# The fourth GEMM's operands as float16 pairs from the second token group on

## The chip, the core and the metric

The kernel runs on one NeuronCore of a Trainium2 chip. TensorE multiplies, VectorE, ScalarE and GpSimd (POOL) do the elementwise work, and SyncE's queue (SP) issues every DMA. The metric is the device time of one execution in microseconds: before the change 741.53 us, the median of three runs (739.75 to 742.87).

## The reference

The computation is one attention block and two feed-forward blocks behind it, on 2304 tokens:

```python
out = attention(q_l, k_l, v_l, q_g, k_g, v_g)        # 4 batches, 8 heads of 64: 512 local tokens with a window of 32, 32 global ones
x   = out as (2304, 512)
h   = x @ w_in                                        # GEMM 1, (512, 1024)
s   = h * softmax(h);  ln = (s - mean) / sqrt(var + 1e-6) * g_ln
x   = ln @ w_out                                      # GEMM 2, (1024, 512)
h   = x @ w2_in                                       # GEMM 3, (512, 2048)
g   = h * clip(h + 3, 0, 6) / 6
out = g @ w2_out                                      # GEMM 4, (2048, 512)
```

All inputs are float32, and the weight matrices come as 64-bit words of which the kernel takes out the float32 values on chip ("decoding").

## The kernel before

**Numbers as pairs.** GEMMs 1 to 3 are done in float16 with each operand as a pair: a high half (the value, scaled by a power of two and rounded) and a low half (the rest). A product takes three passes: high by high, high by low, low by high. GEMM 4 works in the same three passes with pairs of float32r, which need no scale: the pair of `w2_out` (tile w2o, made in `prep_w2` by L887 and L354) and the pair of g (tile gr, made by L914 and L916).

**Tiling.** The tokens are 17 tiles of 128. The last two GEMMs (`second`) run over five groups of 4, 4, 3, 3 and 3 tiles, and in each group over 16 blocks f of 128 of the 2048 hidden columns. For a block, GEMM 3 puts 12 matmuls (3 passes by 4 parts of the depth, L906, 512 or 384 moving columns) into one of two PSUM banks S. From there ScalarE makes the clipped factor (L910), VectorE the product g (L912), ScalarE the high half (L914), VectorE the low half (L916). GEMM 4 (L925) then takes 3 passes by 4 or 3 token tiles, each a matmul with 512 moving columns, into four banks (V_71, V_72, Y_74, Y_75) that collect over all 16 blocks. At the end of a group the banks are scaled by 1/6 (L939 on VectorE, L941 on ScalarE) and written out.

**Weights.** `prep_w2` decodes a block's part of `w2_in` and of `w2_out`. A block of words lands in one of three buffers raw, is taken apart by ScalarE (L404) and VectorE or GpSimd (L410 to L422) into one of five buffers wd (for four early blocks into the memory zone), and is split. The scale of `w2_in` comes from a sum of squares on ScalarE (L428, `norm`, which writes its squares into a tile junk) and a matmul of one column with a matrix of ones (L372, into bank H, `power_scale`), behind which VectorE cuts out the exponent (L368 to L370) and makes the block's factor (L879, tile inv). A block's words come in behind one another through raw, so the decoding of 16 blocks runs beside the end of GEMMs 1 and 2 and beside group 0.

**Order.** A planner (`Plan.schedule`) fixes the order of all instructions on all engines. It takes each operation's cost from formulas such as `dve` and `act`, starts what can start earliest and, among what starts within 0.05 us, the operation of lowest rank. Decoding has ranks up to 56, group 0 from 100 to 118, group 1 from 120 on. A region (the memory of a stage) may be used once the operations of the regions named by `closes` are done. Each engine then runs its list in order: a waiting instruction holds up all that stand behind it on its engine.

## Time and profile before

| | us |
|---|---|
| median of three runs | 741.53 |
| the profiled execution | 739.12 |
| its span, first to last instruction | 737.3 |
| TensorE busy | 681.0 (92%) |
| VectorE busy | 435.4 (59%) |
| ScalarE busy | 391.2 (53%) |
| GpSimd busy | 161.9 (22%) |

Busy times are from the profile's page. Matmuls are pipelined, so their listed durations overlap, and a busy TensorE says only that something was in flight. How fast it goes is read from starts: from the start of one matmul, or of one run of them, to that of the next. The attention and GEMM 1 take the first half; from about 374 us to the end TensorE works on GEMMs 3 and 4, group 0 to about 455 us.

### The profile page before, as it was taken

To read this page: it belongs to the slowest core of one execution; us is meant where nothing else is said; L and a number is where in the kernel's file an instruction comes from. 1 tells how busy PE (TensorE), PEld (TensorE's weight loads), DVE (VectorE), ACT (ScalarE), POOL (GpSimd) and SP (SyncE) were. 2 spreads that over 40 slices of the span, in tenths; PEclk is the share of its full clock that TensorE was granted. 3 is DMA by queue.
4 is the path that set the end of the run, shared out by engine and by line. 5 is a ranking of instruction groups with operands and counts; after the bars stand their busy time and mean duration, and the time that the engine had idled before them with its cause. 6 is when DMAs were issued, how large, how long until landed. Compare 5 with 4: busy or idle time off the path is not lost.

```text
span 737.3 us, 11841 instructions
## 1 busy us (share of the span) xinstructions
PE 681.0 (92%) x4484; PEld 466.2 (63%) x4484; DVE 435.4 (59%) x1052; ACT 391.2 (53%) x736; POOL 161.9 (22%) x192
## 2 busy tenths in 40 slices
PE   3667599999989999898999999999999999999997
...
DVE  4898977877757988868789962231232232223222
...
PEclk9977759999999999999999999999999999999999
...
GB/s 319 243 252 169 217 152 184 156 214 186 224 218 166 183 227 161 146 141 138 177 65 154 125 29 57 1 1 0 1 58 1 0 44 1 0 1 44 1 0 44
DMA packets 155657, 82.93 MB, mean 112 GB/s; under 512 B 132944, under 2 KB 141136, under 8 KB 155600
## 3 DMA queue, kind: packets, MB, share of 16 engines
...
## 4 chain that ended last, share of the span: by engine, by line
PE 70%; DMA 12%; DVE 10%; issue 2%; ACT 2%; SPq 2%; POOL 1%; ACTq 0%; DVEq 0%
PE S L906 20%; PE V L925 14%; PE Y L925 9%; PE Y L852 8%; PE H L792 7%; DMA PT<-zone 7%; PE S L601 5%; PE S L636 2%; DMA lT<-l 2%; PE V L728 2%; DMA vs<-v 2%; DVE wd L417 1%; DMA zone<-in_ki_dram 1%; DVE wd L410 1%; PE V L678 1%
## 5 line engine op out<-in xcount | busy, mean ns | idle before, releaser
L925 PE MATMUL V<-w2o,gr 128*128 128x512 f32 x480 | 155.5, 408 | 0.2 <-ACT gr L914 0.2
L912 DVE SCALAR_TENSOR_TENSOR g<-g,S 128x384 f32<-128x384 f32 (+1 forms) x80 | 48.3, 606 | 158.7 <-ACT g L910 156.5
L906 PE MATMUL S<-ybig,w2i 128*128 128x384 f16 (+1 forms) x720 | 139.7, 348 | 0.5 <-DVE g L912 0.5
L910 ACT ACTIVATE g<-S,three,inv 128x384 f32<-128x384 f32 (+1 forms) x80 | 57.0, 712 | 156.0 <-PE S L906 153.6
L925 PE MATMUL Y<-w2o,gr 128*128 128x512 f32 x336 | 116.0, 397 | 0.0
L906 PEld LDWEIGHTS <-w2i 128*128 128x128 f16 x720 | 67.6, 98 | 65.0 <-issue 10.4
L925 PEld LDWEIGHTS V<-w2o,gr 128*128 128x128 f32 x480 | 88.4, 188 | 23.7 <-ACT gr L914 3.5
L852 PE MATMUL Y<-lT,wout 128*128 128x256 f16 (+1 forms) x864 | 96.6, 269 | 4.5 <-DMA lT<-l 3.2
L792 PE MATMUL H<-win,xT 128*128 128x512 f16 x384 | 91.9, 387 | 0.2 <-DVE tm L805 0.2
L852 PEld LDWEIGHTS <-wout 128*128 128x128 f16 x864 | 79.9, 99 | 18.2 <-DMA lT<-l 4.0
L916 DVE SCALAR_TENSOR_TENSOR gr<-g,inv,gr 128x384 fp32r<-128x384 f32 (+1 forms) x80 | 53.7, 671 | 47.6 <-ACT gr L914 33.2
L914 ACT ACTIVATE gr<-g,inv 128x384 fp32r<-128x384 f32 (+1 forms) x80 | 52.4, 657 | 44.2 <-DVE g L912 44.0
L925 PEld LDWEIGHTS Y<-w2o,gr 128*128 128x128 f32 x336 | 63.2, 188 | 15.5 <-DVE gr L916 0.2
L792 PEld LDWEIGHTS <-xT 128*128 128x128 f16 x384 | 36.6, 100 | 42.5 <-issue 6.6
L601 PE MATMUL S<-zone 64*128 64x224 f32 x256 | 57.4, 454 | 4.9 <-ACT sg L642 4.3
L611 ACT ACTIVATE e<-e,sa 128x224 f32<-128x224 f32 x128 | 52.7, 471 | 9.3 <-DVE sa L606 9.2
L601 PEld LDWEIGHTS S<-zone 64*128 64x128 f32 x256 | 38.8, 230 | 16.2 <-ACT sg L642 6.0
L606 DVE CUSTOM_DVE_ANT_0 e<-msk,S 128x224 f32<-128x224 f32 x128 | 43.1, 382 | 8.6 <-PE S L601 8.3
L906 PE MATMUL S<-ybig,zone 128*128 128x384 f16 (+1 forms) x240 | 47.1, 348 | 0.0
L678 PE MATMUL V<-v,PT 128*128 128x65 f16 x128 | 25.8, 205 | 18.9 <-DMA PT<-zone 18.8
L636 PE MATMUL S<-zone 128*128 128x128 f32 (+1 forms) x128 | 28.0, 352 | 11.6 <-DVE sa L606 11.6
L626 DVE SCALAR_TENSOR_TENSOR zone<-e,zone 128x896 f16<-128x896 f32 x32 | 34.6, 1084 | 3.1 <-ACT zone L624 2.8
(181 smaller groups left out, 1032.2 us busy)
## 6 DMA issues: line engine op xcount, KB each, us to landing
...
```

The source lines that it names most:

```text
L601: T.matmul(out=S()[:, j], lhsT=p.tile(qk)[d, 2 * hf + j], rhs=p.tile(kk)[d, 2 * hf + j], start=True, stop=True)
L606: V.tensor_tensor_reduce(out=p.tile(ek)[:, KC * (2 * j + jj):KC * (2 * j + jj) + KC], in0=msk[:, mtyp], in1=S()[:, j], scale=-0.125, scala ...
L611: A.activation(out=p.tile(ek)[:, c:c + KC], in_=p.tile(ek)[:, c:c + KC], func=AF.Exp, bias=p.tile(sa)[:, h:h + 1], scale=-1.0)
L636: T.matmul(out=p.tile(gk)[:, 0:n], lhsT=p.tile(gq)[:, 2 * hf + j], rhs=p.tile(kk)[:, 2 * hf + j, 0:n], start=(j == 0), stop=(j == 1))
L792: T.matmul(out=p.tile(hk)[:, 512 * n:512 * n + 512], lhsT=(p.tile(xk) if xb else xgT)[:, 4 * a + k], rhs=win16[:, w, k, 512 * n:512 * n + ...
L852: T.matmul(out=Y()[:, m2], lhsT=wout16[:, w, k, 128 * m:128 * m + 128], rhs=p.tile(lk)[:, 8 * a + k, 0:n], start=(z == 0 and k == 0), stop ...
L906: T.matmul(out=p.tile(hk)[:, 0:n], lhsT=p.tile(wk)[:, w, k], rhs=y16[:, a, k, c0:c0 + n], start=(z == 0 and k == 0), stop=(z == 2 and k == 3))
L910: aop(act(n, 2), lambda hk=hk, gk=gk, iv=iv: A.activation(out=p.tile(gk)[:, 0:n], in_=p.tile(hk)[:, 0:n], func=AF.Relu, bias=three, scale= ...
L912: vop(dve(n), lambda hk=hk, gk=gk: V.scalar_tensor_tensor(out=p.tile(gk)[:, 0:n], in0=p.tile(gk)[:, 0:n], scalar=6.0, in1=p.tile(hk)[:, 0: ...
L914: aop(act(n, 1, sbuf=True), lambda rk=rk, gk=gk, iv=iv: A.activation(out=p.tile(rk)[:, 0, 0:n], in_=p.tile(gk)[:, 0:n], func=AF.Copy, scal ...
L916: vop(dve(n, 1), lambda rk=rk, gk=gk, iv=iv: V.scalar_tensor_tensor(out=p.tile(rk)[:, 1, 0:n], in0=p.tile(gk)[:, 0:n], scalar=iv[:, 0:1], ...
L925: T.matmul(out=p.tile(accs[t]), lhsT=p.tile(rk)[:, a, 128 * t:128 * t + 128], rhs=p.tile(ok)[:, w], start=(f == 0 and z == 0), stop=(f == ...
```

## The change

Group 0 stays as it is. From group 1 on GEMM 4 works in float16 pairs: the weights from new tiles wh, and g from a new tile gh, whose two halves are made by the same two instructions as before.

For that, `prep_w2` takes one more sum of squares on ScalarE for each block of `w2_out`. `token_scale` makes one scale for g out of two columns that GEMM 1's normalisation now keeps (lsq, lfac). `convert_scale` adds the 16 sums, sends them through one more matmul with ones and makes 16 factors. `convert` turns each block's float32r pair into a float16 pair: the high half on ScalarE, the rest in two steps on VectorE, of which the first writes over the high float32r half and so stands behind group 0's use of it. The pairs go into the memory of the decoding (raw, wd, four parts of the zone, junk), which is free when the last block is decoded. Outputs of groups 1 to 4 are scaled by a column (inv6) instead of a constant, and there is one output buffer less.

```diff
-    tags(const, "raw", SLOTS["raw"], [128, 1024], F32)
-    tags(const, "wd", SLOTS["wd"], [128, 512], F32)
+    tags(const, "raw", SLOTS["raw"], [128, 1024], F32, "r")
+    tags(const, "wd", SLOTS["wd"], [128, 512], F32, "r")
...
-        carve(f"wz{f}", 1, [128, DM], F32, "z")
+        carve(f"wz{f}", 1, [128, DM], F32, "zr")
...
+    halves = [t[:, z:z + DM] for t in p.slots["raw"]["tiles"] for z in (0, 512)] + [t[:, 0:DM] for t in p.slots["wd"]["tiles"]]
+    halves += [t for f in range(SLOTS["EARLY"], SLOTS["EARLY"] + SLOTS["ZONE"]) for t in p.slots[f"wz{f}"]["tiles"]]
+    halves = [t.bitcast(F16) for t in halves] + [junk.bitcast(F16)]
+    for f in range(NF):
+        p.tag(f"wh{f}", [halves[f].rearrange("p (a n) -> p a n", a=2)], "c")
...
         aop(act(512, sbuf=True), lambda: A.activation(out=p.tile(o2)[:, 0], in_=p.tile(d2), func=AF.Copy), r=[d2], w=[("w2oh", f)], b=[d2, o2], rank=rank + 0.05)
+        norm(lambda: p.tile(d2), am_w2o[:, f:f + 1], [d2, ("inv3", f)], "amw2o", rank + 0.06, [d2], scale=ivk[:, 0:1])
...
+    def token_scale(rank):
+        t = const.tile([128, NU + 1], F32, name="tsc")
+        si = g_scale.bitcast(I32)
+        pk = p.buf("tsc", "H")
+        x = t[:, 0:NU]
+        steps = [
+            lambda: V.scalar_tensor_tensor(out=x, in0=lfac, scalar=2.0 ** -30, in1=lfac, op0=ALU.mult, op1=ALU.mult),
+            lambda: V.tensor_tensor(out=x, in0=x, in1=lsq, op=ALU.mult),
+            lambda: V.tensor_tensor(out=x, in0=x, in1=x, op=ALU.mult),
+            lambda: V.tensor_tensor(out=x, in0=x, in1=x, op=ALU.mult),
+            lambda: V.tensor_reduce(out=t[:, NU:NU + 1], in_=x, axis=AX.X, op=ALU.add),
+        ]
...
+        pe(0.12, lambda: T.matmul(out=p.tile(pk)[:, 0:1], lhsT=ones, rhs=t[:, NU:NU + 1], start=True, stop=True), r=prev, w=["tsc5"], b=[pk], rank=rank)
...
+    def convert_scale(rank):
+        vop(dve(NF), lambda: V.tensor_reduce(out=am_w2o[:, NF:NF + 1], in_=am_w2o[:, 0:NF], axis=AX.X, op=ALU.add), r=["amw2o"], w=["amw2o1"], rank=rank)
+        s = power_scale(lambda: am_w2o[:, NF:NF + 1], ["amw2o1"], "s_w2o", rank, "H")
+        vop(0.07, lambda: V.tensor_scalar(out=inv6, in0=s[:, 1:2], scalar1=g_scale[:, 1:2], scalar2=1.0 / 6.0, op0=ALU.mult, op1=ALU.mult), r=["s_w2o", "g_scale"], w=["inv6"], rank=rank)
+        for f in range(NF):
+            vop(0.13, lambda f=f: V.tensor_scalar(out=inv3[f][:, 1:2], in0=inv3[f][:, 0:1], scalar1=s[:, 0:1], scalar2=None, op0=ALU.mult), r=["s_w2o", ("inv3", f)], w=[("wt", f)], rank=rank + 0.1 * f)
+
+    def convert(f, rank):
+        ok = ("w2o", f)
+        hk = p.buf(("wh", f), f"wh{f}")
+        iv = inv3[f]
+        done = [("o", 0, f, 2)] if f < NF - 1 else [("oo", 0, t) for t in range(GROUPS[0][1])]
+        aop(act(512, 1, sbuf=True), lambda: A.activation(out=p.tile(hk)[:, 0], in_=p.tile(ok)[:, 0].bitcast(F32), func=AF.Copy, scale=iv[:, 1:2]),
+            r=[ok, ("wt", f)], w=[("whh", f)], b=[ok, hk], rank=rank)
+        vop(dve(512, 1), lambda: V.scalar_tensor_tensor(out=p.tile(ok)[:, 0], in0=p.tile(ok)[:, 0].bitcast(F32), scalar=iv[:, 1:2], in1=p.tile(hk)[:, 0], op0=ALU.mult, op1=ALU.subtract),
+            r=[("whh", f)] + done, w=[("wht", f)], b=[ok, hk], rank=rank)
+        vop(dve(512, 1), lambda: V.scalar_tensor_tensor(out=p.tile(hk)[:, 1], in0=p.tile(ok)[:, 1].bitcast(F32), scalar=iv[:, 1:2], in1=p.tile(ok)[:, 0].bitcast(F32), op0=ALU.mult, op1=ALU.add),
+            r=[("wht", f)], w=[hk], b=[ok, hk], rank=rank)
...
-            rk = p.buf(("gr", gi, f), "gr")
-            wk, ok = ("w2i", f), ("w2o", f)
+            rk = p.buf(("gr", gi, f), "gh" if gi else "gr")
+            wk, ok = ("w2i", f), ("wh" if gi else "w2o", f)
...
+            gs, own = (g_scale[:, 0:1], ["g_scale"]) if gi else (iv[:, 0:1], [])
...
+            sc, ptr, need = (inv6, 1, ["inv6"]) if gi else (1.0 / 6.0, 0, [])
...
     for gi in range(len(GROUPS)):
         second(gi)
+        if gi == 0:
+            token_scale(100.0)
+            convert_scale(115.9)
+            for f in range(NF):
+                convert(f, 118.0 + f)
...
-    p.schedule({"g": ["a"], "h": ["m"], "z": ["s"]})
+    p.schedule({"g": ["a"], "h": ["m"], "z": ["s"], "zr": ["s"], "c": ["r", "zr"]})
...
-            shapes = {"g": ([128, 512], F32), "gr": ([128, 2, 512], F32R), "o": ([128, DM], F32)}
+            shapes = {"g": ([128, 512], F32), "gr": ([128, 2, 512], F32R), "gh": ([128, 2, 512], F16), "o": ([128, DM], F32)}
```

The planner makes a new order for all engines. Up to about 320 us TensorE's and VectorE's lists are as before. On ScalarE, in the decoding of the last blocks, stood before, between the sums of squares for the `w2_in` scales of blocks 14 and 15 (inv_14, inv_15; w2o_4214 is block 14's pair, g and gr are the steps of blocks 11 and 12):

```order
L428 ACTIVATE junk,inv_14_202<-wd_90 128x512
L887 ACTIVATE w2o_4214<-wd_86 128x512
L910 ACTIVATE g_3517<-S_69,three,inv_12_198 128x512
L441 ACTIVATE wd_90<-wd_90,psc_203 128x512
L404 ACTIVATE wd_88<-raw_85 128x512
L447 ACTIVATE w2i_3537<-wd_90 128x512
L914 ACTIVATE gr_3521<-g_3519,inv_11_196 128x512
L428 ACTIVATE junk,inv_15_204<-wd_87 128x512
```

and now:

```order
L436 ACTIVATE junk,inv_14_207<-wd_90 128x512
L901 ACTIVATE w2o_4235<-wd_86 128x512
L449 ACTIVATE wd_90<-wd_90,psc_208 128x512
L455 ACTIVATE w2i_3546<-wd_90 128x512
L436 ACTIVATE junk,am_w2o<-wd_86,inv_14_207 128x512
L436 ACTIVATE junk,inv_15_209<-wd_87 128x512
```

The steps of blocks 11 and 12 have moved behind; the new sum of squares of block 14 (into am_w2o) stands in front of block 15's.

On TensorE, around the one-column matmul for block 15's scale (H_73 from inv_15), GEMM 4 of blocks 10 (w2o_4210) and 11 (w2o_4211) stood before:

```order
L925 MATMUL Y_74<-w2o_4210,gr_3520 128x512
L925 MATMUL Y_75<-w2o_4210,gr_3520 128x512
L372 MATMUL H_73<-inv_15_204,ones 128x1
L925 MATMUL V_71<-w2o_4211,gr_3521 128x512
L925 MATMUL V_72<-w2o_4211,gr_3521 128x512
```

and now GEMM 3 of block 13 (w2i_3545) in front of it and GEMM 4 of block 9 (w2o_4230) behind it, with the token scale's matmul:

```order
L968 LDWEIGHTS w2i_3545
L968 MATMUL S_70<-ybig,w2i_3545 128x512
L372 MATMUL H_73<-inv_15_209,ones 128x1
L988 MATMUL V_71<-w2o_4230,gr_3529 128x512
L988 MATMUL V_72<-w2o_4230,gr_3529 128x512
L988 MATMUL Y_74<-w2o_4230,gr_3529 128x512
L988 MATMUL Y_75<-w2o_4230,gr_3529 128x512
L926 MATMUL H_73<-tsc,ones 128x1
```

Twenty matmuls more of GEMM 4 now stand behind that matmul.

On VectorE, at the end of group 0, the steps of blocks 12 to 15 stood before without anything between them (inv_12 to inv_15 name the blocks):

```order
L916 SCALAR_TENSOR_TENSOR gr_3520<-g_3517,inv_12_198,gr_3520 128x512
L912 SCALAR_TENSOR_TENSOR g_3518<-g_3518,S_70 128x512
L916 SCALAR_TENSOR_TENSOR gr_3521<-g_3518,inv_13_200,gr_3521 128x512
L912 SCALAR_TENSOR_TENSOR g_3519<-g_3519,S_69 128x512
L916 SCALAR_TENSOR_TENSOR gr_3520<-g_3519,inv_14_202,gr_3520 128x512
L912 SCALAR_TENSOR_TENSOR g_3517<-g_3517,S_70 128x512
L916 SCALAR_TENSOR_TENSOR gr_3521<-g_3517,inv_15_204,gr_3521 128x512
L912 SCALAR_TENSOR_TENSOR g_3518<-g_3518,S_69 128x512
```

and now, behind the matmul for the common scale, the first conversion (w2o_92 with raw_83 is block 0) and the steps of blocks 14 and 15, with the last two of the 16 factors ahead:

```order
L937 TENSOR_SCALAR inv_14_207<-inv_14_207,psc_212 128x1
L937 TENSOR_SCALAR inv_15_209<-inv_15_209,psc_212 128x1
L946 SCALAR_TENSOR_TENSOR w2o_92<-w2o_92,inv_0_179,raw_83 128x512
L979 SCALAR_TENSOR_TENSOR gr_3528<-g_3527,inv_14_207,gr_3528 128x512
L948 SCALAR_TENSOR_TENSOR raw_83<-w2o_92,inv_0_179 128x512
L974 SCALAR_TENSOR_TENSOR g_3525<-g_3525,S_70 128x512
L946 SCALAR_TENSOR_TENSOR w2o_3548<-w2o_3548,inv_1_181,raw_83 128x512
L946 SCALAR_TENSOR_TENSOR w2o_4223<-w2o_4223,inv_2_183,raw_84 128x512
L979 SCALAR_TENSOR_TENSOR gr_3529<-g_3525,inv_15_209,gr_3529 128x512
L948 SCALAR_TENSOR_TENSOR raw_83<-w2o_3548,inv_1_181 128x512
```

Conversions and the steps of g take turns on VectorE from here to block 4 of group 1.

## Rows read from the trace of the kernel before

**Rows 1.** The page, 40 slices, tenths: TensorE busy, VectorE busy, granted clock.

```profile
PE   3667599999989999898999999999999999999997
...
DVE  4898977877757988868789962231232232223222
...
PEclk9977759999999999999999999999999999999999
```

**Rows 2.** The page, the chain that ended last, by engine.

```profile
PE 70%; DMA 12%; DVE 10%; issue 2%; ACT 2%; SPq 2%; POOL 1%; ACTq 0%; DVEq 0%
```

**Rows 3.** Windows: length, busy us (count) of PE, PEld, DVE, ACT, POOL; clock, DMA, GB/s.

```profile
340.00:350.00 10.00, 7.81 (x43) 4.21 (x41) 9.33 (x21) 6.01 (x10) 3.27 (x4) 0.95 1.07 225
350.00:360.00 10.00, 10.00 (x84) 8.54 (x83) 7.71 (x15) 4.40 (x8) 0.00 (x0) 0.88 0.45 142
...
420.00:430.00 10.00, 10.00 (x46) 6.40 (x46) 9.82 (x19) 7.46 (x14) 3.51 (x3) 1.00 0.19 60
430.00:440.00 10.00, 10.00 (x47) 6.46 (x46) 4.66 (x12) 2.80 (x5) 1.71 (x1) 1.00 0.01 2
```

**Rows 4.** The chain in order of time: start us, us, what.

```profile
360.16 6.11 DMA lT<-l
...
467.86 5.19 PE S L906 x24
478.69 5.20 PE S L906 x24
...
563.19 3.92 PE S L906 x24
571.32 3.92 PE S L906 x24
```

**Rows 5.** Lines by form from 455 us on: busy us, mean ns, idle before.

```profile
L925 PE MATMUL V<-w2o,gr 128*128 128x512 f32 x385 | 124.0, 406 | 0.0
L925 PE MATMUL Y<-w2o,gr 128*128 128x512 f32 x240 | 86.0, 397 | 0.0
...
L925 PEld LDWEIGHTS V<-w2o,gr 128*128 128x128 f32 x384 | 71.0, 188 | 18.3 <-ACT gr L914 2.2 <-ACT o L941 0.3
L906 PEld LDWEIGHTS <-w2i 128*128 128x128 f16 x564 | 53.2, 98 | 46.6 <-issue 6.8
...
L914 ACT ACTIVATE gr<-g,inv 128x512 fp32r<-128x512 f32 x15 | 10.8, 723 | 11.3 <-DVE g L912 11.3
```

**Rows 6.** Timeline, end of group 0: start us, us, engine, line, what.

```profile
453.52 1.57 PE L925 MATMUL V<-w2o,gr 128*128 128x512 f32 x6
```

**Rows 7.** Timeline, TensorE and ScalarE in the decoding.

```profile
423.25 0.63 ACT L428 ACTIVATE junk<-wd 128x512 bf16<-128x512 f32 x1 [0.43 <-DVE wd L419]
...
423.88 0.61 ACT L887 ACTIVATE w2o<-wd 128x512 fp32r<-128x512 f32 x1
...
430.23 0.28 PE L372 MATMUL H<-inv,ones 128*128 128x1 f32 x2
...
430.92 0.63 PE L925 MATMUL Y<-w2o,gr 128*128 128x512 f32 x2
```

**Rows 8.** Waits of TensorE from 320 to 455 us: total, times, longest.

```profile
PE H L372 <- ACT junk L428: 1.8, 2, 1.6
...
PE Y L852 <- DMA lT<-l: 1.3, 2, 0.7
PE S L906 <- DVE g L912: 0.5, 1, 0.5
```

**Rows 9.** Timeline, VectorE at the end of the decoding.

```profile
431.84 0.20 DVE L879 TENSOR_SCALAR inv<-psc,psc 128x1 f32<-128x1 f32 x1
...
431.97 0.68 DVE L419 SCALAR_TENSOR_TENSOR wd<-raw,wd 128x512 int32<-128x512 int32 x1
...
432.57 0.74 DVE L437 SCALAR_TENSOR_TENSOR w2i<-wd,psc,w2i 128x512 f16<-128x512 f32 x1
...
433.23 0.74 DVE L916 SCALAR_TENSOR_TENSOR gr<-g,inv,gr 128x512 fp32r<-128x512 f32 x1
```

More of the change, by code (lines that the diff above doesn't have):

```diff
@@ L774, in passes @@
         return [[(k, a, w) for k in range(n)] for a, w in ((0, 0), (0, 1), (1, 0))]
+    lsq = const.tile([128, NU], F32, name="lsq")
+    lfac = const.tile([128, NU], F32, name="lfac")
     def gemm1(u):
@@ L806, in gemm1 @@
             port=False, r=[("me", u)], w=[("mu", u)], b=[hk, uk, tk], rank=rank)
-        aop(act(1024, 1, 1, True), lambda: A.activation(out=junk, in_=p.tile(uk), func=AF.Square, bias=c(3), scale=-float(DFF), accum_out=c(5)),
+        aop(act(1024, 1, 1, True), lambda: A.activation(out=junk, in_=p.tile(uk), func=AF.Square, bias=c(3), scale=-float(DFF), accum_out=lsq[:, u:u + 1]),
             r=[("mu", u)], w=[("sq", u)], b=[uk, tk], rank=rank)
@@ L814, in gemm1 @@
         tiny(lambda: G.tensor_scalar(out=c(7), in0=c(6), scalar1=c(6), scalar2=1e-6 * DFF * 2.0 ** -10, op0=ALU.mult, op1=ALU.mult), ["c6"], "c7")
-        tiny(lambda: G.tensor_scalar(out=c(8), in0=c(5), scalar1=2.0 ** -30, scalar2=c(7), op0=ALU.mult, op1=ALU.add), ["sq", "c7"], "c8")
-        tiny(lambda: G.tensor_tensor(out=c(9), in0=c(8), in1=mhalf, op=ALU.pow), ["c8"], "y3", 0.5)
+        tiny(lambda: G.tensor_scalar(out=c(8), in0=lsq[:, u:u + 1], scalar1=2.0 ** -30, scalar2=c(7), op0=ALU.mult, op1=ALU.add), ["sq", "c7"], "c8")
+        tiny(lambda: G.tensor_tensor(out=lfac[:, u:u + 1], in0=c(8), in1=mhalf, op=ALU.pow), ["c8"], "y3", 0.5)
         mode = MODE["l"][u]
@@ L824, in gemm1 @@
                r=[("sq", u)], w=[("mc", u)], b=[uk, tk], rank=rank)
-        aop(act(1024, 1, 0, True), lambda: A.activation(out=p.tile(lk)[:, 0], in_=p.tile(uk), func=AF.Copy, scale=c(9)),
+        aop(act(1024, 1, 0, True), lambda: A.activation(out=p.tile(lk)[:, 0], in_=p.tile(uk), func=AF.Copy, scale=lfac[:, u:u + 1]),
             r=[("mc", u), ("y3", u)], w=[("lh", u)], b=[uk, lk, tk], rank=rank)
-        vop(dve(1024, 1), lambda: V.scalar_tensor_tensor(out=p.tile(lk)[:, 1], in0=p.tile(uk), scalar=c(9), in1=p.tile(lk)[:, 0], op0=ALU.mult, op1=ALU.subtract),
+        vop(dve(1024, 1), lambda: V.scalar_tensor_tensor(out=p.tile(lk)[:, 1], in0=p.tile(uk), scalar=lfac[:, u:u + 1], in1=p.tile(lk)[:, 0], op0=ALU.mult, op1=ALU.subtract),
             r=[("lh", u)], w=[lk], b=[uk, lk, tk], rank=rank)
@@ L864, in attention_solu_swish_kernel @@
     w2i, w2o, inv3 = {}, {}, {}
+    am_w2o = const.tile([128, NF + 1], F32, name="am_w2o")
+    inv6 = const.tile([128, 1], F32, name="inv6")
     three = const.tile([128, 1], F32, name="three")
@@ new lines, in token_scale @@
+    def token_scale(rank):
[10 more added lines that the diff above has]
+        ]
+        prev = [("y3", u) for u in range(NU)]
+        for z, fn in enumerate(steps):
+            vop(dve(NU), fn, r=prev, w=[("tsc", z)], rank=rank)
+            prev = [("tsc", z)]
+        pe(0.12, lambda: T.matmul(out=p.tile(pk)[:, 0:1], lhsT=ones, rhs=t[:, NU:NU + 1], start=True, stop=True), r=prev, w=["tsc5"], b=[pk], rank=rank)
+        vop(0.13, lambda: V.tensor_scalar(out=si[:, 2:3], in0=p.tile(pk).bitcast(I32)[:, 0:1], scalar1=26, scalar2=23, op0=ALU.logical_shift_right, op1=ALU.logical_shift_left), port=False, r=["tsc5"], w=["tsc6"], b=[pk], rank=rank)
+        vop(0.07, lambda: V.tensor_scalar(out=si[:, 0:1], in0=si[:, 2:3], scalar1=-1.0, scalar2=float(128 << 23), op0=ALU.mult, op1=ALU.add), r=["tsc6"], w=["g_scale"], rank=rank)
+        vop(0.07, lambda: V.tensor_scalar(out=si[:, 1:2], in0=si[:, 2:3], scalar1=1.0, scalar2=float(126 << 23), op0=ALU.mult, op1=ALU.add), r=["tsc6"], w=["g_scale"], rank=rank)
```

21 lines of the change are left out of this document (12 added, 9 removed).

## The prediction

> **What bounds the kernel now.** I read the page from the top: busy shares, the 40 slices, the chain of waits; then a table of ten-microsecond windows, then the chain in order of time, and last the lines grouped by form and the timeline. TensorE is busy 92% of the span, and in the slices it stands at 9 from 350 us to the last but one, while VectorE falls to between 1 and 3 in the last sixteen [rows 1]. TensorE has 70% of the chain that ended last [rows 2]. The granted clock's digit is 9 there throughout, the upper of its two levels (2.4 GHz) [rows 1]. So two stretches matter. From about 455 us to the end the kernel is bound by TensorE's own rate. From 374 to 433 us, where the weights of the last GEMMs are decoded beside token group 0, TensorE and VectorE are both full: 10.00 and 9.82 us of ten, with ScalarE at 7.46; after 430 VectorE drops to 4.66 [rows 3], because the decoding is over, while TensorE has 20 us of group 0 still to do: its last matmuls start at 453.52 [rows 6].
>
> **The rate of the fourth GEMM, and what float16 gives.** In the chain, GEMM 3 of two blocks (24 float16 matmuls of 512 columns) takes 5.20 us, 0.2163 each, and the next such run begins 10.83 us after the last (467.86, 478.69). What lies between is GEMM 4 of two blocks, 24 float32r matmuls, also of 512 columns: 5.63 us, 0.2347 each. In the groups of three tiles 24 matmuls of 384 columns take 3.92 us and the period is 8.13 (563.19, 571.32), which leaves 4.21 us for 18 float32r matmuls, 0.2339 each [rows 4]. The weight load of a float32r matmul is 188 ns against 98 in float16 [rows 5]; at either rate it is shorter than the matmul it hides behind, so the longer load is at most part of the 18 ns. That the cause is not the turning through four accumulators: where three matmuls in a row go into one bank, six take 1.57 us, and with the last one's 0.39 off that is 0.236 each [rows 6].
>
> If GEMM 4 ran at GEMM 3's pitch, a pair of blocks in group 1 would take 48 x 0.2163 = 10.38 us, 0.45 less than 10.83; eight pairs give 3.6 us. In groups 2 to 4 a pair would take 3.92 + 18 x 0.2163 = 7.81, 0.32 less than 8.13; 24 pairs give 7.6 us. Together **11.2 us** off, for 624 matmuls (the lines count 385 + 240 from 455 us on, one of them group 0's [rows 5]). Taking the whole difference of one steady stretch and the first matmul behind each change of format, I get no more than 12.0, and with steady pitches alone 10.9: those are its bounds if the format is the cause at all.
>
> The Trainium skill ("TensorE: Matmul & The Clock Gate", section "Back-to-back issue gap") gives the spacing of warm matmuls as a function of the columns alone, 216 ns at 512. The float16 rows agree with it (216); the float32r rows do not (234). By that rule alone the two formats would cost the same and the change would gain nothing, which is the third case below.
>
> **What is added on TensorE.** Two one-column float32 matmuls with the matrix of ones, for the token scale and for the common weight scale. One of that kind holds the queue: from 430.23 to 430.92 a pair of GEMM 4 matmuls and one such step take 0.69 us, the pair alone 0.47 [rows 7]: 0.22 each, **0.4 us**. It can't be less than nothing and not more than 0.8 (a full load and pass each).
>
> **What is added in the decoding.** Sixteen sums of squares on ScalarE, one for each block of the second weight matrix. The same step without a scale operand takes 0.63 us from its start to the next one's (423.25 to 423.88 [rows 7]), and a copy with one such operand takes 723 ns [rows 5], so 0.72 at most each, 11.5 us in all. Five of them (blocks 0 to 4) fall between 300 and 350 us; there TensorE waits for transposes of the normalised rows, which the chain shows as DMA (360.16, 6.11 us long [rows 4]) and which can start only when the one lT buffer is free. Behind that wait I count nothing; without it they would cost up to 3.6 us. (The matmul for block 5's scale moves behind 96 matmuls of GEMM 2. It made TensorE wait 1.6 us for a sum of squares, the larger part of the 1.8 in [rows 8]; what is late next is the lT transpose, for which TensorE waits right behind it (0.7 at most [rows 8]), so I count nothing as won.) Blocks 5 to 7 are likewise before 374 us. Blocks 8 to 15 fall into the stretch where VectorE is full; eight times 0.72 is 5.8 us of ScalarE, which has 2.5 us of ten free [rows 3], so in sum they fit. In order they don't quite: TensorE's waits there were down to 0.5 us for one g [rows 8], the queues are tight. The new order of TensorE shows one place: between the matmuls for the scales of blocks 14 and 15 it now has one GEMM 3 block, 12 x 0.216 = 2.6 us, where before it had 20 GEMM 4 matmuls and 4 of GEMM 3, 5.6 us. ScalarE meanwhile goes through a copy, a scaling, a copy, the new sum of squares of block 14 and then that of block 15's first weights: five steps of 0.6 to 0.7 and a wait of some 0.4 for VectorE's scale, 3.7 us. TensorE stands about **1.1 us** there; with 0.4 more for the same kind of delay at blocks 8 to 13, **1.5 us**. Bounds: 0 (all hidden) and 5.8 (each of the eight exposed in full).
>
> **The handover from group 0 to group 1.** The common scale needs the sum over all 16 blocks, so its matmul stands behind GEMM 4 of block 13; the last sum of squares is long there (decoding ends near 433 us [rows 9], group 0 some 20 us later with three blocks behind that point), so the matmul itself waits for nothing. Behind it on VectorE stand 16 one-column factors at 0.13 us, then 32 conversions of 512 columns, each 0.66 us to the next start (432.57 to 433.23, duration 0.74; a g step 0.60 [rows 9]): 21 us, among the g and gr steps of blocks 14 and 15 and of group 1. ScalarE gets 16 more steps of 0.6. I walked both queues from that matmul (time 0) with these steps. Block 14's high half comes at 3.8 us and its low half at 4.8; TensorE, which has 20 matmuls of GEMM 3 first, wants them at 4.3 and 5.2. Block 15 is complete at 8.5, wanted at 8.9; block 0 of group 1 at 12.8 and 13.5, wanted at 13.4 and 14.3; block 4, the last behind a row of conversions, at 32.6 and 33.8, wanted at 33.4 and 34.3. TensorE has work in front of it each time, by margins of 0.4 to 0.9 us; I take **0.5 us** for what slips. Bounds: 0, and 4 (if the 42 VectorE steps up to block 4 take their durations, 0.09 more each, 3.8 us). From block 5 on the conversions are done, and ScalarE and VectorE have the load that they had before.
>
> Evacuating with a scale operand instead of a constant adds 0.1 us to the last output, and nothing elsewhere. One output buffer less: three or four are written every 65 to 87 us.
>
> **The sum.** -11.2 + 0.4 + 1.5 + 0.5 + 0.1 = -8.7 us. Against the profiled execution (737.3 us of span, 739.12 in all) that is 730.4; against the median of the runs, 741.53, it is **732.8**. The profiled one lies 2.4 under the median and inside the runs' spread of 3.1, so the forecast is made from the median.
>
> **The rivals.** A change under 0.5% (3.7 us: 737.8 to 745.2) can't be told from none.
>
> First, the forecast: TensorE-bound behind 455 us, small losses in front. 732.8, its own range 730 to 736.5. For it: the runs of GEMM 3 follow each other in the chain at these two periods [rows 4].
>
> Second, both upper bounds in front of it: -11.2 + 0.4 + 5.8 + 4 + 0.1 = -0.9, 740.6. For it: VectorE at 98% and ScalarE in lockstep with it up to 430 us. Against: the 20 us of TensorE work that are left when decoding ends.
>
> Third, the change doesn't do what it says: the 18 ns stay in float16, because they come from what GEMM 4 reads. Then only the costs are left: 741.5 + 2.5 = 744.0, no change. Against: the load's own time and the one-bank row above, and that GEMM 3's and GEMM 4's matmuls otherwise have the same shape.
>
> Fourth, slower: ScalarE is what holds the decoding, and all 16 sums of squares come out in full on TensorE, 11.5 us, and take the clock with them. The trace has such a place: TensorE waits 2.2 us between 340 and 350 us, and the granted clock is 0.95 and 0.88 in that window and the next [rows 3], a loss of 10 x 0.05 + 10 x 0.12 = 1.7 us, 0.77 per microsecond waited. 11.5 x 1.77 = 20.4; -11.2 + 0.4 + 0.5 + 0.1 + 20.4 = +10.2, 751.7. It decides from 13.9 us of such loss on. Against: ScalarE is not full anywhere in the stretch.
>
> **Chances and range.** Forecast 0.79, second 0.12, third 0.05, fourth 0.04. The second case spreads from 736.5 on, and about half of it lies under 737.8; with what the forecast has above it, faster comes to 0.85, within 0.5% to 0.10, slower to 0.05. The range that leaves a fifth out reaches from 729.0 (the gain at its upper bound, losses near nothing) to 738.0, into the second case.
>
> **What will show it.** In the chain, the periods of 10.83 and 8.13 us become about 10.38 and 7.81. If they stay, the third case holds. The wait of the block-15 scale matmul for a sum of squares appears with about 1 us. TensorE has no wait over 0.5 us between 440 and 490 us; several such, or a granted clock under 1.00 there, speak for the second case, a clock under 1.00 between 374 and 440 for the fourth. The start of group 1's first GEMM 4 block, set against group 0's last, tells how much was lost in front. The forecast is wrong if less than 9 us of the gain shows behind 455 us, or more than 4 us are lost before.

## The result, and the profile after

The changed kernel takes 731.65 us, the median of four runs (728.81 to 732.84), against 740.64 (738.04 to 742.87) for the kernel before on the same chip: a ratio of 0.9874 with an interval of [0.9828, 0.9920], 9.0 us less. The profiled execution took 730.79 us, 729.0 of them span. That is 1.2 under the forecast of 732.8 and inside its range of 729.0 to 738.0. Not all of the steps were as I had put them.

Line numbers have moved: GEMM 3 is L968 (before L906), GEMM 4 L988 (L925), the clipped factor L972 (L910), g L974 (L912), its halves L977 and L979 (L914, L916), GEMM 2 L864 (L852), the sums of squares L436 (L428). The conversions are L944, L946 and L948, the common scale's factors L937. An experiment that adds lines moves these numbers by one to four; the tile names tell which step a row is.

The page first: 40 slices in tenths of TensorE, of VectorE and of the granted clock, then the chain that ended last, by engine. They answer to [rows 1, 2].

```profile
PE   3667689999999999899899989999999999999997
...
DVE  4898877878757988786879996943232322323322
PEclk9998758999999999999999999999999999999999
...
PE 72%; DMA 11%; DVE 9%; ACT 3%; SPq 2%; issue 2%; POOL 0%; DVEq 0%; POOLq 0%; ACTq 0%
```

TensorE is still the bound and the granted clock is at its upper level from 374 us on. VectorE, which fell off at 430 us before, is full once more in the slice from about 456 us on: the conversions.

The chain in order of time (start us, us, what), for [rows 4]:

```profile
361.24 6.76 DMA lT<-l
368.05 5.52 PE Y L864 x96
...
491.09 5.18 PE S L968 x24
501.45 5.18 PE S L968 x24
...
561.71 3.90 PE S L968 x24
569.50 3.90 PE S L968 x24
```

The periods are 10.36 and 7.79 us, where they were 10.83 and 8.13; forecast were 10.38 and 7.81. Between two runs of GEMM 3 are 10.36 - 5.18 = 5.18 us for 24 matmuls of GEMM 4, 0.2158 each: in float16 GEMM 4 goes at GEMM 3's own pitch. The clock is not the difference: it is 1.00 between 500 and 510 us in both kernels. Nor is it the place of the weights, which lie in other memory now: two matmuls start 0.43 us behind the last two, whether the weights come from raw, wd or the zone. Its lines by form from 455 us on (busy us, mean ns, idle before), for the L925 lines of [rows 5]:

```profile
L988 PEld LDWEIGHTS <-gh 128*128 128x128 f16 x624 | 60.6, 98 | 71.7 <-ACT gh L977 3.6 <-DVE gh L979 0.5
```

All 624 are float16, and the load is down from 188 to 98 ns. The waits of TensorE between 320 and 455 us (total, times, longest), for [rows 8]:

```profile
PE Y L864 <- DMA lT<-l: 4.1, 2, 2.8
PE S L968 <- DVE g L974: 2.7, 3, 1.7
...
PE S L372 <- ACT junk L436: 0.6, 1, 0.6
```

Here is the first surprise. The wait that I had put at the matmul for block 15's scale is not in the list (the 0.6 us at L372 belong to a matmul of an early block, into bank S at 340 us), and GEMM 3 waits 2.7 us for g instead (0.5 before). The timeline shows where (start us, us, engine, line, what, the idle time in front and who ended it):

```profile
418.86 2.75 PE L968 MATMUL S<-ybig,w2i 128*128 128x512 f16 x12 [0.41 <-DVE g L974]
...
426.94 2.75 PE L968 MATMUL S<-ybig,w2i 128*128 128x512 f16 x12 [1.68 <-DVE g L974]
429.53 0.28 PE L372 MATMUL H<-inv,ones 128*128 128x1 f32 x2
...
433.49 1.89 PE L968 MATMUL S<-ybig,w2i 128*128 128x512 f16 x8 [0.56 <-DVE g L974]
...
455.86 1.54 PE L988 MATMUL V<-w2o,gr 128*128 128x512 f32 x6
```

The matmul for block 15's scale (429.53) starts without a wait. GEMM 3 of block 13, in front of it, had to wait 1.68 us for its PSUM bank, which is free when VectorE has made g of block 11 from it. VectorE's own queue just before that:

```profile
425.48 0.69 DVE L417 SCALAR_TENSOR_TENSOR wd<-raw,wd 128x512 int32<-128x512 int32 x1
426.09 0.14 DVE L369 TENSOR_SCALAR psc<-psc 128x1 int32<-128x1 int32 x1
426.15 0.14 DVE L370 TENSOR_SCALAR psc<-psc 128x1 int32<-128x1 int32 x1
426.21 0.68 DVE L974 SCALAR_TENSOR_TENSOR g<-g,S 128x512 f32<-128x512 f32 x1
```

The g step ends at 426.89 and the matmuls start at 426.94; in front of it stands decoding, without a gap. In the new order TensorE runs three blocks of GEMM 3 nearly in a row there, with VectorE's g steps behind decoding steps. Between 445 and 500 us TensorE's list of waits is empty.

**Where the time went.** Two marks divide the span: the start of GEMM 2's last 96 matmuls, and the last run of six GEMM 4 matmuls of group 0 into V (453.52 in [rows 6], 455.86 now). The orders are alike around both, but for four GEMM 3 matmuls (4 x 0.216 = 0.87 us) that stood in front of the second mark before and stand behind it now; the kernel before is corrected for them.

| us | first mark | between the marks | behind the second |
|---|---|---|---|
| before | 366.31 | 86.34 | 284.65 |
| before, profiled again | 370.99 | 86.65 | 284.76 |
| changed | 368.05 | 87.81 | 273.14 |
| changed, again | 368.97 | 88.22 | 273.11 |

The decoding and the rest of group 0 have lost 1.2 to 1.9 us, and what lies behind has won 11.5 to 11.7. The first column is mostly scatter: one and the same kernel differs by 4.7 us there. Its last 45 us can be had apart from that, from the four one-column matmuls at about 322 us, up to which TensorE's lists are alike, to the first mark. Before the change (the first two rows) and after it:

```profile
321.45 0.50 PE L372 MATMUL S<-inv,ones 128*128 128x1 f32 x4
...
366.31 5.52 PE L852 MATMUL Y<-lT,wout 128*128 128x128 f16 x96 [0.72 <-DMA lT<-l]
```

```profile
321.77 0.50 PE L372 MATMUL S<-inv,ones 128*128 128x1 f32 x4
...
368.05 5.52 PE L864 MATMUL Y<-lT,wout 128*128 128x128 f16 x96 [1.24 <-DMA lT<-l]
```

That is 44.86 us before (profiled again 44.68, from 326.31 to 370.99) and 46.28 after (again 45.60, from 323.37 to 368.97): 0.7 to 1.6 us lost here too. The waits for the transposes lT, 4.1 us now, were 1.3 before, and the 1.6 us for a sum of squares that stood in front of them are gone [rows 8].

### The profile page after: what moved, and what is told of

Same layout as the page of the kernel before. It is cut to its first block, busy times and chain, and to the rows that moved or that the text cites. A ratio compares the mean times of both kernels' runs of the same rounds, so it can differ in the third digit from the quotient of the medians.

```text
span 729.0 us, 11979 instructions
## 1 busy us (share of the span) xinstructions
PE 670.0 (92%) x4488; PEld 415.0 (57%) x4488; DVE 459.7 (63%) x1113; ACT 411.8 (56%) x784; POOL 162.9 (22%) x192
## 4 chain that ended last, share of the span: by engine, by line
PE 72%; DMA 11%; DVE 9%; ACT 3%; SPq 2%; issue 2%; POOL 0%; DVEq 0%; POOLq 0%; ACTq 0%
PE S L968 20%; PE V L988 13%; PE Y L988 9%; PE Y L864 9%; PE H L804 9%; DMA PT<-zone 5%; PE S L609 5%; DMA lT<-l 2%; PE S L644 2%; PE V L736 2%; DMA wd<-in_vm_dram 2%; DVE wd L417 1%; DVE wd L410 1%; DVE e L614 1%; DMA zone<-in_qi_dram 1%
## 5 line engine op out<-in xcount | busy, mean ns | idle before, releaser
L968 PE MATMUL S<-ybig,w2i 128*128 128x384 f16 (+1 forms) x720 | 139.5, 347 | 2.7 <-DVE g L974 2.7
L972 ACT ACTIVATE g<-S,three,inv 128x384 f32<-128x384 f32 (+1 forms) x80 | 57.0, 712 | 134.3 <-PE S L968 132.4
L974 DVE SCALAR_TENSOR_TENSOR g<-g,S 128x384 f32<-128x384 f32 (+1 forms) x80 | 48.2, 605 | 122.9 <-ACT g L972 120.6
L968 PEld LDWEIGHTS <-w2i 128*128 128x128 f16 x720 | 70.0, 98 | 65.9 <-issue 5.4
L864 PE MATMUL Y<-lT,wout 128*128 128x256 f16 (+1 forms) x864 | 97.3, 271 | 7.2 <-DMA lT<-l 5.9
L988 PEld LDWEIGHTS <-gh 128*128 128x128 f16 x624 | 60.6, 98 | 71.7 <-ACT gh L977 3.6
L864 PEld LDWEIGHTS <-wout 128*128 128x128 f16 x864 | 80.1, 99 | 21.6 <-DMA lT<-l 6.6
L979 DVE SCALAR_TENSOR_TENSOR gh<-g,g_scale,gh 128x384 f16<-128x384 f32 (+1 forms) x64 | 41.7, 651 | 41.9 <-ACT gh L977 27.6
L977 ACT ACTIVATE gh<-g,g_scale 128x384 f16<-128x384 f32 (+1 forms) x64 | 41.0, 641 | 41.0 <-DVE g L974 41.0
L968 PE MATMUL S<-ybig,zone 128*128 128x384 f16 (+1 forms) x240 | 47.2, 347 | 0.0
L988 PE MATMUL V<-raw,gh 128*128 128x512 f16 x144 | 42.8, 379 | 0.0
L988 PE MATMUL V<-wd,gh 128*128 128x512 f16 x120 | 35.7, 379 | 0.0
L968 PEld LDWEIGHTS <-zone 128*128 128x128 f16 x240 | 23.4, 99 | 20.5 <-issue 0.3
```

What stands on the lines that cost most here:

```text
L864: T.matmul(out=Y()[:, m2], lhsT=wout16[:, w, k, 128 * m:128 * m + 128], rhs=p.tile(lk)[:, 8 * a + k, 0:n], start=(z == 0 and k == 0), stop ...
L968: T.matmul(out=p.tile(hk)[:, 0:n], lhsT=p.tile(wk)[:, w, k], rhs=y16[:, a, k, c0:c0 + n], start=(z == 0 and k == 0), stop=(z == 2 and k == 3))
L972: aop(act(n, 2), lambda hk=hk, gk=gk, iv=iv: A.activation(out=p.tile(gk)[:, 0:n], in_=p.tile(hk)[:, 0:n], func=AF.Relu, bias=three, scale= ...
L974: vop(dve(n), lambda hk=hk, gk=gk: V.scalar_tensor_tensor(out=p.tile(gk)[:, 0:n], in0=p.tile(gk)[:, 0:n], scalar=6.0, in1=p.tile(hk)[:, 0: ...
L977: aop(act(n, 1, sbuf=True), lambda rk=rk, gk=gk, gs=gs: A.activation(out=p.tile(rk)[:, 0, 0:n], in_=p.tile(gk)[:, 0:n], func=AF.Copy, scal ...
L979: vop(dve(n, 1), lambda rk=rk, gk=gk, gs=gs: V.scalar_tensor_tensor(out=p.tile(rk)[:, 1, 0:n], in0=p.tile(gk)[:, 0:n], scalar=gs, in1=p.ti ...
```

## The experiments

**1. The changed kernel again**, as the measure for the next three.

> The changed kernel once more, beside the three others on one chip. Theory (float16 takes 18 ns off each of 624 matmuls, the additions cost about 3 us): 8 to 9.5 us under the kernel before, periods in the chain 10.36 and 7.785 us again, and TensorE's waits for a g between 410 and 435 us again 2 to 3 us in all. Rival (the 1.7 us that the changed kernel lay behind at 373 us was this one execution's own): GEMM 2 ends within 0.7 us of the 371.8 us of before.

731.41 us (730.27 to 732.12) against 741.7 (737.69 to 743.98, 17 runs): ratio 0.9855 [0.9827, 0.9883]. That is 10.3 us less, more than the 8 to 9.5 expected; the periods are 10.36 and 7.78 us and the waits for g are again 2.7 us in 3.

**2. All that is added, without float16 matmuls.** GEMM 4 stays in float32r in all groups; sums, scales and conversions are made and not used. Two of the places changed:

```diff
...
-        mm4c = mm16(512) if gi else mm32(512)
+        mm4c = mm32(512)
...
-            wk, ok = ("w2i", f), ("wh" if gi else "w2o", f)
+            wk, ok = ("w2i", f), ("w2o", f)
...
```

> All additions kept (16 sums of squares, token scale, common scale, 48 conversion steps), but GEMM 4 of all groups works in float32r as before; the conversions write their result where nothing reads it, and outputs are scaled by the constant. Theory: periods 10.83 and 8.13 us as before; 2.5 to 3.5 us above the kernel before, 11 to 12 above the changed one. Rival 1 (the new order or the freed waits bring part of the gain): below the kernel before. Rival 2 (the additions are hidden, and the matmuls bring 9, not 11): within 1 us of the kernel before.

743.91 us, ratio 1.0035 [1.0016, 1.0055]: above the kernel before by 2.2 us between the medians and by 2.6 by the ratio, with 1.2 to 4.1 in the interval, and 12.5 between the medians above the changed kernel. The chain keeps the old periods:

```profile
496.64 5.20 PE S L968 x24
507.46 5.20 PE S L968 x24
...
562.14 3.92 PE S L968 x24
570.23 3.92 PE S L968 x24
```

The periods are 10.82 and, over five periods, 8.11. Between the marks it has 88.24 us, 1.6 to 1.9 more than before; behind the second 284.03, 0.6 to 0.7 less than before (its periods are 0.01 to 0.02 shorter) and 10.9 more than the changed kernel. From the four matmuls at 322 us (325.81 here) to the first mark (371.73) it takes 45.92 us, 1.1 to 1.2 more than before. So the additions together cost about the 2.5 us forecast, though part of it where nothing was counted, and the float16 operands alone carry the gain. Nothing waits for the conversions in this kernel, so it tests the time they take on the engines and not the handover.

**3. The 16 sums of squares left out, the order kept.** The common scale comes from a constant instead of them, which one added memset on VectorE sets at the start; otherwise no engine's list changes but ScalarE's.

```diff
+    V.memset(am_w2o, 2.0 ** -24)
...
-        norm(lambda: p.tile(d2), am_w2o[:, f:f + 1], [d2, ("inv3", f)], "amw2o", rank + 0.06, [d2], scale=ivk[:, 0:1])
+        aop(act(512, 1, 1, True), lambda: None, r=[d2, ("inv3", f)], w=["amw2o"], b=[d2], rank=rank + 0.06)
```

> The changed kernel without its 16 new sums of squares (a constant of the same size stands for them, so the common scale comes out the same); the order of everything else on all engines is that of the changed kernel. Theory (they delay ScalarE, and through it the g steps that free the S banks): TensorE's waits for a g between 410 and 435 us fall from 2.7 to under 1.3 us, and the time is 1 to 2 us under the changed kernel's. Rival (the waits come from the order itself, in which VectorE's g steps stand behind decoding steps): waits stay over 2 us, time within 0.7 us of the changed kernel.

729.09 us, ratio 0.9824 [0.9794, 0.9853]. Its waits of TensorE between 320 and 455 us:

```profile
PE Y L864 <- DMA lT<-l: 3.5, 2, 2.4
PE S L969 <- DVE g L975: 2.5, 3, 1.7
...
```

The waits for g stay, 2.5 for 2.7, with no sum of squares on ScalarE. So they come from the order, as the rival had it, and not from ScalarE's time. Between the marks are 87.63 us, 0.2 to 0.6 less than in the changed kernel: that is what the sums themselves cost there. The 2.3 us between the medians are more than the 0.7 that the rival allowed, though the intervals overlap. Part of the rest lies in front of the first mark:

```profile
325.04 0.50 PE L372 MATMUL S<-inv,ones 128*128 128x1 f32 x4
...
369.96 5.52 PE L864 MATMUL Y<-lT,wout 128*128 128x128 f16 x96 [1.07 <-DMA lT<-l]
```

These 44.92 us are again those of the kernel before (44.68 and 44.86), with the order of the changed kernel (45.60 and 46.28). So in this one profile what was lost there goes with the sums, and not with the order.

**4. The last eight sums behind the decoding.** Blocks 8 to 15 are summed in a row once all are decoded, and the planner makes another order.

```diff
-        norm(lambda: p.tile(d2), am_w2o[:, f:f + 1], [d2, ("inv3", f)], "amw2o", rank + 0.06, [d2], scale=ivk[:, 0:1])
+        if f < 8:
+            norm(lambda: p.tile(d2), am_w2o[:, f:f + 1], [d2, ("inv3", f)], "amw2o", rank + 0.06, [d2], scale=ivk[:, 0:1])
...
     def convert_scale(rank):
+        for f in range(8, NF):
+            norm(lambda f=f: p.tile(("w2o", f))[:, 0].bitcast(F32), am_w2o[:, f:f + 1], [("w2oh", f), ("w2oh", NF - 1), ("inv3", f)], "amw2o", 99.0, [("w2o", f)], scale=inv3[f][:, 0:1])
```

> The sums of squares of blocks 8 to 15 taken from the float32r high half, in one row behind the last block's decoding, where ScalarE idles; the planner orders anew. Theory: the decoding stretch runs as before the change, waits for a g under 1 us, 0.5 to 1.5 us under the changed kernel. Rival (the new order is as tight in another place, or the row of eight delays block 13's g): as the changed kernel within 0.5 us.

732.47 us (730.22 to 733.36), ratio 0.9868 [0.9839, 0.9897]. The waits:

```profile
PE H L372 <- DVE am_w2o L936: 0.6, 1, 0.6
...
PE S L971 <- DVE g L977: 0.5, 1, 0.5
```

With this order the waits for g are 0.5 us again, as before the change, at the price of one of 0.6 for the common scale. From the first mark to the end it takes 359.9 us, 1.1 to 1.4 less than the changed kernel (361.0 and 361.3), but the whole time is 1.1 above the changed kernel's by the medians, with runs that overlap, so no gain is shown. It is no version to prefer on these runs.

The next six kernels ran once each and are read by their rows.

**5 to 7. Why float32r is slower.** Do the 18 ns belong to each instruction or its longer weight load, or to each column that streams? Three kernels: the kernel before with each GEMM 4 matmul cut into two of 256 columns (a load each), the changed kernel cut in the same way, and the kernel before with only 64 of the 128 weight columns loaded in groups 1 to 4, which leaves out the outputs of half their tokens. The cut, in both kernels:

```diff
-                        T.matmul(out=p.tile(accs[t]), lhsT=p.tile(rk)[:, a, 128 * t:128 * t + 128], rhs=p.tile(ok)[:, w], start=(f == 0 and z == 0), stop=(f == NF - 1 and z == 2))
+                        for q in range(2):
+                            T.matmul(out=p.tile(accs[t])[:, 256 * q:256 * q + 256], lhsT=p.tile(rk)[:, a, 128 * t:128 * t + 128], rhs=p.tile(ok)[:, w, 256 * q:256 * q + 256], start=(f == 0 and z == 0 and q == 0), stop=(f == NF - 1 and z == 2 and q == 1))
```

The 64 weight columns:

```diff
-                        T.matmul(out=p.tile(accs[t]), lhsT=p.tile(rk)[:, a, 128 * t:128 * t + 128], rhs=p.tile(ok)[:, w], start=(f == 0 and z == 0), stop=(f == NF - 1 and z == 2))
+                        T.matmul(out=p.tile(accs[t])[0:(64 if gi else 128)], lhsT=p.tile(rk)[:, a, 128 * t:128 * t + (64 if gi else 128)], rhs=p.tile(ok)[:, w], start=(f == 0 and z == 0), stop=(f == NF - 1 and z == 2))
```

> The kernel before with each GEMM 4 matmul of 512 moving columns cut into two of 256, each with its own weight load, in float32r, in all groups. What are the 18 ns by which a float32r matmul of 512 columns is slower? Theory A (the load of 188 ns is hidden behind the matmul, but some 18 to 20 ns of every float32r load are not): a matmul of 256 then is bound by its load, 188 + 20 = 205 to 215 ns. Theory B (the moving float32r columns are slower, 4% each): bound by the load alone, 186 to 192 ns. Either way GEMM 4 takes 150 to 180 ns more per pair and the kernel 120 to 145 us more.

> The changed kernel with the same cut: two matmuls of 256 columns in float16 from group 1 on (group 0 in float32r). The load is 98 ns. If a float16 matmul is bound by its columns, 256 take half of the 216, about 109 ns, and groups 1 to 4 are as long as in the changed kernel; if part of its load shows as well, 115 to 125 ns, and those groups are 4 to 10 us longer. Group 0 is longer by some 192 x 0.16 to 0.18 = 31 to 35 us in both cases.

> The kernel before, in which GEMM 4 of groups 1 to 4 loads only 64 of the 128 weight columns (and so leaves out half of the tokens' outputs). The moving side is unchanged: 512 float32r columns. Theory A (part of the load is not hidden): the pitch falls from 0.234 toward 0.225 or less, if that part is in proportion to the columns loaded. Theory B (the moving columns): it stays 0.234. If the unhidden part of a load is a constant, it stays 0.234 too, and the run with 256 columns has to tell.

The chain of the first, and its float32r loads from 460 us on by form:

```profile
491.60 5.20 PE S L906 x24
502.45 5.20 PE S L906 x24
...
565.59 3.92 PE S L906 x24
573.73 3.92 PE S L906 x24
```

```profile
L926 PEld LDWEIGHTS V<-w2o,gr 128*128 128x128 f32 x757 | 103.2, 189 | 3.7 <-ACT gr L914 2.2
```

The period hardly moves, 10.85 and 8.14: 48 matmuls of 256 columns in 5.65 us, 0.1177 each. A load is listed with 189 ns, and yet one follows the other every 118. So the loads overlap, and their listed length bounds nothing here. The numbers expected of this kernel rested on loads that do bound a matmul of 256 columns; they were wrong on either theory: it took 742.49 us, where 738.45 was measured beside it for the kernel before and 120 to 145 more had been expected. In float16 the cut gives 10.42 and 7.83 in groups 1 to 4, as expected (what was expected of group 0, still in float32r, did not come, for the same reason):

```profile
507.71 5.18 PE S L968 x24
518.13 5.18 PE S L968 x24
...
568.32 3.90 PE S L968 x24
576.15 3.90 PE S L968 x24
```

(10.42 - 5.18) / 48 = 0.1092 per matmul. Set side by side: float32r 0.1177 and 0.2347 us for 256 and 512 columns, which is 0.457 ns for each column and 0.7 on top; float16 0.1092 and 0.2158, 0.416 ns for each column and 2.6 on top. The difference is 8.5 ns at 256 columns and 18.9 at 512: it grows with the columns that stream. A cost that is the same for every instruction or every load, as the whole cause, is out. With 64 weight columns, of which the chain shows:

```profile
491.48 5.20 PE S L906 x24
502.15 5.19 PE S L906 x24
```

the period is 10.67, 0.228 per matmul: 6.5 ns less, between what the two theories had (0.225 and 0.234). So about a third of the difference goes with half of the weight columns, and half of the outputs with them. Why a column takes longer in float32r, and why fewer weight columns help, no run here shows; that stays open.

**8. The kernel before, profiled again.**

> The kernel before, profiled once more. Up to some 320 us all its lists are those of the changed kernel, whose GEMM 2 ended 1.7 us later than here. If that is scatter between executions of the first half: the end of GEMM 2 lies anywhere from 371 to 375 us, and the time from the start of its last 96 matmuls to the end of the span is again within 0.5 us of 371.0. If it is a cost of the change: within 0.5 us of 371.8.

744.14 us. The first mark is at 370.99 instead of 366.31, and what lies behind is alike to 0.4 us (the table above); GEMM 2 ends at about 376 us, outside even the 371 to 375 expected. A loss of 1 or 2 us in the first half can therefore not be read from when the first mark comes, only from a row shortly in front of it, as above.

**9. The handover's margin.** The second VectorE step of each conversion is done twice, the order kept: by plan 16 x 0.66 = 10.6 us more on VectorE behind group 0, by the busy times of the pages 11.6 (471.3 against 459.7).

```diff
+        def two():
+            for _ in range(2):
+                V.scalar_tensor_tensor(out=p.tile(hk)[:, 1], in0=p.tile(ok)[:, 1].bitcast(F32), scalar=iv[:, 1:2], in1=p.tile(ok)[:, 0].bitcast(F32), op0=ALU.mult, op1=ALU.add)
-        vop(dve(512, 1), lambda: V.scalar_tensor_tensor(out=p.tile(hk)[:, 1], in0=p.tile(ok)[:, 1].bitcast(F32), scalar=iv[:, 1:2], in1=p.tile(ok)[:, 0].bitcast(F32), op0=ALU.mult, op1=ALU.add),
+        vop(dve(512, 1), two,
```

> The changed kernel with the second VectorE step of each conversion done twice (same result, same order of all instructions on all engines): 16 x 0.66 = 10.6 us more VectorE work between group 0's end and block 5 of group 1. Theory (the handover fits by margins of 0.4 to 0.9 us, as walked): each block of group 1 up to block 4 now comes later than TensorE wants it, so TensorE waits several times between 450 and 490 us, 5 to 9 us in all, and the part of the span behind the start of GEMM 2's last 96 matmuls grows from 361.0 to 366-370. Rival (the handover has far more room than walked, so nothing was risked): waits under 1 us in all, that part stays at 361 to 362.

From group 0's last six V matmuls to those of group 1 it takes 95.40 us (459.59 to 554.99), where the changed kernel takes 84.29 (455.86 to 540.15): 11.1 more. The waits between 445 and 500 us, of which the changed kernel has none, and three windows (length, busy us and count of PE, PEld, DVE, ACT, POOL; clock, DMA, GB/s):

```profile
PE V L991 <- ACT gh L980: 3.6, 1, 3.6
PE S L971 <- DVE g L977: 2.2, 1, 2.2
PE V L991 <- ACT o L1008: 1.4, 1, 1.4
```

```profile
470.00:480.00 10.00, 6.38 (x23) 2.38 (x21) 9.89 (x15) 2.11 (x3) 0.00 (x0) 0.83 0.01 2
480.00:490.00 10.00, 7.79 (x35) 3.39 (x34) 9.82 (x16) 2.17 (x3) 0.00 (x0) 0.95 0.00 0
490.00:500.00 10.00, 10.00 (x43) 4.25 (x41) 6.70 (x10) 1.77 (x3) 0.00 (x0) 0.88 0.00 0
```

7.2 us of waits, and behind them a clock of 0.83, 0.95 and 0.88, part of the time at the lower level (1.2 GHz), another 10 x (0.17 + 0.05 + 0.12) = 3.4. Together 10.6 of the 11.1. I had expected 5 to 9 us of waits for the theory and had left the clock out, so the part from the first mark on, 372.4 us, is above the 366 to 370 expected. VectorE is at 98% there: the handover fits, but with no more room than was walked. At block 1 of group 1, which I had not listed, there is less: its GEMM 4 starts 1.49 us behind its g step in this run, after a wait (472.62 to 474.11), and 1.52 us behind it in the changed kernel, without one (463.51 to 465.03).

**10. The margin of the sums.** Each new sum of squares is taken twice, the order kept: 11.6 us more on ScalarE by the busy times of the pages (423.4 against 411.8).

```diff
+    spare = const.tile([128, NF], F32, name="spare")
...
-        norm(lambda: p.tile(d2), am_w2o[:, f:f + 1], [d2, ("inv3", f)], "amw2o", rank + 0.06, [d2], scale=ivk[:, 0:1])
+        def two(d2=d2, f=f, ivk=ivk):
+            for col in (spare[:, f:f + 1], am_w2o[:, f:f + 1]):
+                A.activation(out=junk[:, 0:512], in_=p.tile(d2), func=AF.Square, scale=ivk[:, 0:1], accum_out=col)
+        aop(act(512, 1, 1, True), two, r=[d2, ("inv3", f)], w=["amw2o"], b=[d2], rank=rank + 0.06)
```

> The changed kernel with each of the 16 new sums of squares taken twice (same order): 16 x 0.6 to 0.7 = 10 us more ScalarE work in the decoding. Theory (the 1 us that I had put at the block-15 scale matmul was not there because the order, not ScalarE's time, makes TensorE wait; the sums are covered): the part behind the start of GEMM 2's last 96 matmuls stays at 361 to 363, and the start of these is within the scatter of 366 to 371.7. Rival (ScalarE's time is what delays the decoding, and the changed kernel is just under the edge): eight exposed sums, 5.8 us, that part 366 to 367, with waits of TensorE for ScalarE between 374 and 440.

The rival's case came out, 0.5 us above its 366 to 367: 367.5 us from the first mark to the end (739.5 - 372.03), 6.1 to 6.5 more than in the changed kernel, all of it between the marks (94.31 us there). GEMM 2's last 96 matmuls in the timeline, and the waits of TensorE from 370 to 445 us:

```profile
372.03 7.15 PE L864 MATMUL Y<-lT,wout 128*128 128x128 f16 x96 [2.26 <-DMA lT<-l]
```

```profile
PE S L972 <- DVE g L978: 2.7, 3, 1.6
...
PE H L372 <- ACT junk L436: 2.1, 4, 0.7
PE V L992 <- ACT gr L981: 1.4, 3, 0.7
```

The 2.7 for g are as ever; 2.1 + 1.4 = 3.5 us of waits for ScalarE are new, four of them at the scale matmuls. The 96 matmuls take 7.15 us instead of 5.52, with a granted clock of 0.83 between 370 and 380 us: 1.6 more. These 1.6 need not come from the second set. The kernel of experiment 6, with a single set, has them too, likewise behind some 2 us of waiting for lT:

```profile
371.31 7.15 PE L864 MATMUL Y<-lT,wout 128*128 128x128 f16 x96 [1.95 <-DMA lT<-l]
```

Waits and clock make 5.1 of the 6.1 to 6.5; the rest I did not find. So between the marks one set of sums costs 0.2 to 0.6 us and the second 4.5 to 6.5: the decoding was just under the edge. My theory, that the order alone sets these waits, holds for the waits for g in the changed kernel and no further.

## Why the prediction was right, and where it wasn't

**The rate.** -11.2 us were forecast for 624 matmuls. Behind the second mark it is 11.5 to 11.7 less than before, 10.9 less than in experiment 2. The third case, that the 18 ns stay, fell with the periods. The Trainium skill ("TensorE: Matmul & The Clock Gate", section "Back-to-back issue gap") gives the spacing of isolated warm matmuls as the columns over 2.4 GHz and 2.5 ns, with no term for the format. The float16 rows agree with it at both widths (0.2158 and 0.1092 us), the float32r rows at neither (0.2347, 0.1177), and the measurement decides. For streams of load and matmul pairs, which is what runs here, the same section of the Trainium skill has about 131 ns at 512 columns. The prediction left that figure out, and no row here shows it, in either format. I was also right that the weight load is not the cause, though my reason, that 188 ns are shorter than the matmul, was the weaker one: experiment 5 shows loads listed as longer than the matmul, and no loss.

**The decoding.** 1.5 us for the sums and 0.4 for two one-column matmuls were forecast; 1.2 to 1.9 were lost between the marks, in the changed kernel and in experiment 2. The size holds, the step does not: I had put 1.1 us of it at the matmul for block 15's scale, waiting for ScalarE. That matmul waits for nothing. I had read correctly that one block of GEMM 3 stands in front of it now, but had not asked whether that block itself could start: its bank waits for g, 1.68 us, and when it is through, the scale's sum is there. Experiment 3 shows that this wait does not need the sums, and experiment 4 that it goes with the order. So the amount of this step came out right by luck, from another cause.

**The early blocks.** I counted nothing for blocks 0 to 7, because TensorE waits for the transposes lT there anyway. That failed: from 322 us to the first mark the changed kernel takes 0.7 to 1.6 us longer, experiment 2 1.1 to 1.2, and experiment 3, without the sums, no longer than before. The wait for lT does not hide the sums: it is 4.1 us against 1.3 (3.5 in experiment 3), and only 1.6 us of another wait are gone. That the sums delay the normalised rows, and these the transposes, is argued from the order of the steps and not shown. What is lost in front of 322 us, if anything, the scatter hides.

**The handover.** 0.5 us were forecast; the changed kernel has no wait there, and experiment 2, which has all conversions on the engines, shows no loss behind the second mark. That the margins were as small as walked, and smaller at block 1, is shown by experiment 9.

**The rivals.** The second case (740.6) was the kernel with both covers gone. In the changed kernel neither was. Experiments 9 and 10 put about as much work again under one cover each and lose 11 and 4.5 to 6.5 us: both covers are nearly used up. The fourth needed 13.9 us of loss in the decoding; twice the sums gave 7.7 to 8.0 against the kernel before.

**The sum.** -8.7 were forecast, with -9.0 and -10.3 measured in two comparisons. From the four matmuls at 322 us to the end, where one profile can be set against another, it is -8.6 to -9.2 (407.23 and 406.93 us against 415.85 and 416.09). Of that -11.5 to -11.7 lie behind the second mark, where the rate's -11.2 and the handover's 0.5 were forecast; 1.2 to 1.9 lie between the marks, where 1.9 were; and 0.7 to 1.6 lie in front of the first, where I had nothing. That the sum is met so closely is in part luck: a rate a few tenths better and a handover that costs nothing make up for the term that I left out.
